# A cross-attention and GELU kernel: the exponential's table and one block pair moved ahead, one sum and one product moved back

## The chip, the cores and the metric

The kernel runs on one core of one Trainium2 chip. The metric is the device time of one execution in microseconds (us); the figure of a kernel is the median of its runs.

## What is computed

For each of 8 batches and 8 heads, a sequence x (512 rows of 64) and a state (32 rows of 64) read each other by softmax attention. The 544 rows of a batch, heads side by side, then go through two matrix products with an exact GELU between them.

```python
def _attn_ref(x, state):                  # x: (8, 8, 512, 64), state: (8, 8, 32, 64)
    scores = scale * np.matmul(x, state.transpose(0, 1, 3, 2))
    # ... softmax over the 32 states gives a
    xread = np.matmul(a, state)
    scores2 = scale * np.matmul(state, x.transpose(0, 1, 3, 2))
    # ... softmax over the 512 rows gives a2
    sread = np.matmul(a2, x)
    return np.concatenate([xread, sread], axis=2)

def _moe_ref(x, w_in, w_out):             # x: (4352, 512), w_in: (512, 2048), w_out: (2048, 512)
    h = x @ w_in
    g = 0.5 * h * (1.0 + erf(h * inv_sqrt2))
    return g @ w_out
```

## The kernel before

Batches are worked in turn. The kernel never forms xread: it multiplies each head's state by its rows of w_in first (`p_mm`, giving P), and the hidden layer of a batch is then P by the transposed attention weights AT. Block m of 16 is 128 of the 2048 hidden columns (`mm1`, called in pairs by `M(16 * b + m, ...)`), and ScalarE's GELU takes it from PSUM. So a batch needs, in order: its x in SBUF (`load_x`), rearranged by GpSimd (`rearr`) and transposed by a DMA (`xtr_dma`); the scores and their exponential (`scores`); the division by the row sums (`norm`, called "scaling" here); the weights transposed by a DMA (`atr_dma`); then its 16 blocks.

The second product of batch 0 is done in units of four matmuls (`U(12)` to `U(15)` are the last of it). That of later batches is done with seven half-size products in place of eight, after Strassen: VectorE adds quadrants of g (`g_sum`) or of w_out (`w_sums`), and `X(b, name)` is one of the seven products, 16 matmuls each.

PSUM has eight banks. Four form the pool `ps_f`, tag "f", whose tiles are given out in rotation: the fifth tile takes the buffer of the first and waits until it has been read. The other four are named o0 to o3; X's seven products use them as the table in `X` says.

ScalarE holds one function table at a time, so each change between the exponential and GELU brings a table load. Each engine works through its own instructions in the order in which they are written, and engines wait for one another only where data or a buffer is shared. `hold_for` is a tiny copy on GpSimd whose only purpose is that GpSimd, which also issues the loads of x, stands still until some block's GELU is there.

```python
    xin = ctx.enter_context(tc.tile_pool(name="xin", bufs=2))
    att = ctx.enter_context(tc.tile_pool(name="att", bufs=2))
    ps_f = ctx.enter_context(tc.tile_pool(name="ps_f", bufs=4, space=PSUM))
    ps_o = ctx.enter_context(tc.tile_pool(name="ps_o", bufs=1, space=PSUM))
# ... cut ...
    def state_prep(b0, b1, pool=ps_f, tag="f"):
        n = b1 - b0
        ps = pool.tile([128, n, HC, NS], BF16, name="st_ps", tag=tag)
        for b in range(b0, b1):
            nc.tensor.transpose(
                ps[:, b - b0, :, :].rearrange("p c n -> p (c n)"),
                st_bf[:, b, :, :].rearrange("q t d -> q (t d)"),
                ident,
            )
        for t in range(2):
            nc.vector.tensor_copy(
                out=sbd[64 * t:64 * t + 64, b0:b1, :, 32 * t:32 * t + 32].rearrange(
                    "d b c n -> d (b c) n"
                ),
                in_=ps[64 * t:64 * t + 64, :, :, :].rearrange("d b c n -> d (b c) n"),
            )
# ... cut ...
    def rearr(b, ts=(0, 1)):
        A = atts[b]
        src = xbs[b].rearrange("p (t c) (j d) -> p t c j d", t=2, d=D)
        for t in ts:
            nc.gpsimd.tensor_copy(
                out=A.x4[:, :, :, 64 * t:64 * t + 64].rearrange("p j c d -> p c j d"),
                in_=src[:, t],
            )
# ... cut ...
    def xtr_dma(b):
        A = atts[b]
        nc.sync.dma_start_transpose(
            out=A.xT.rearrange("p j c n -> p (j c) n"),
            in_=A.x4.rearrange("p j c n -> p (j c n)"),
        )
# ... cut ...
    def scores(b, half):
        A = atts[b]
        if half == 0:
            begin_e(b)
        pt = ps_f.tile([128, SJ, 2, 2, NS], FP32, name="pt", tag="f")
        for ci in range(2):
            c = 2 * half + ci
            for j in range(SJ):
                nc.tensor.matmul(
                    pt[:, j, :, ci, :],
                    lhsT=A.xT[:, j, c, :],
                    rhs=sbd[:, b, c, :],
                    start=True,
                    stop=True,
                )
        nc.scalar.activation(
            out=A.e[:, :, 64 * half:64 * half + 64],
            in_=pt.rearrange("p j t c n -> p (j t) (c n)"),
            func=AF.Exp,
            scale=scale,
        )
# ... cut ...
    def norm(b, half):
        A = atts[b]
        G = SJ * 2
        hs = slice(64 * half, 64 * half + 64)
        e4 = A.e[:, :, hs].rearrange("p g (c n) -> p g c n", n=NS)
        cs = att.tile([128, G, 2], FP32, name="cs", tag="cs")
        nc.vector.reduce_sum(out=cs, in_=e4, axis=AX.X)
        ics = att.tile([128, G, 2], FP32, name="ics", tag="ics")
        nc.vector.reciprocal(out=ics, in_=cs)
        nc.vector.tensor_tensor(
            out=A.a[:, :, hs].rearrange("p g (c n) -> p g c n", n=NS),
            in0=e4,
            in1=ics[:, :, :].to_broadcast((128, G, 2, NS)),
            op=ALU.mult,
        )
# ... cut ...
    def atr_dma(b):
        A = atts[b]
        A.AT = att.tile([128, SJ, 2, 128], BF16, name="AT", tag="AT")
        nc.sync.dma_start_transpose(
            out=A.AT.rearrange("p j t n -> p (j t) n"), in_=A.a
        )
# ... cut ...
    def p_mm(b, f, tiles):
        if b not in Ps:
            Ps[b] = att.tile([128, 2, d_ff], BF16, name="P", tag="P")
        ps = [tiles([128, 512], "p_ps") for t in range(2)]
        for c in range(HC):
            for t in range(2):
                nc.tensor.matmul(
                    ps[t][32 * c:32 * c + 32, :],
                    lhsT=sbd[64 * t:64 * t + 64, b, c, 32 * t:32 * t + 32],
                    rhs=w_in_bf[64 * t:64 * t + 64, c, f * 512:(f + 1) * 512],
                    start=True,
                    stop=True,
                )
        return ps
# ... cut ...
    def p_copy(b, f, ps):
        dst = Ps[b][:, :, f * 512:(f + 1) * 512]
        nc.scalar.copy(out=dst[:, 0, :], in_=ps[0])
        nc.vector.tensor_copy(out=dst[:, 1, :], in_=ps[1])
# ... cut ...
    def mm1(b, m):
        if m == 0:
            gs[b] = gpool.tile([128, MC, S], BF16, name="g", tag="g")
        hp = ps_f.tile([128, S], FP32, name="hp", tag="f")
        for t in range(2):
            nc.tensor.matmul(
                hp,
                lhsT=Ps[b][:, t, m * 128:(m + 1) * 128],
                rhs=atts[b].AT[:, :, t, :],
                start=(t == 0),
                stop=(t == 1),
            )
        nc.scalar.activation(out=gs[b][:, m, :], in_=hp, func=AF.Gelu)
# ... cut ...
    def g_sum(b, name):
        (h0, k0), (h1, k1), op = G_SUMS[name]
        t = apool.tile([128, MH, 256], BF16, name="gsum", tag="gsum")
        nc.vector.tensor_tensor(out=t, in0=g_q(b, h0, k0), in1=g_q(b, h1, k1), op=op)
        xs[b, "g" + name] = t
# ... cut ...
    def X(b, name):
        bank = {"3": 0, "4": 1, "5": 0, "2": 1, "1": 2, "6": 3, "7": 2}[name]
        first = name in "3416"
        if first:
            xs[b, bank] = otile([128, 2, NH], "xp", bank)
        ps = xs[b, bank]
        lhs = {"3": (0, 0), "4": (1, 1)}.get(name)
        lhs = xs[b, "g" + name] if lhs is None else g_q(b, *lhs)
        rhs = {"5": w_q[1][1], "2": w_q[0][0]}.get(name)
        rhs = w_sum[name] if rhs is None else rhs
        x_mm(ps, lhs, rhs, first)
        if name == "3":
            xs[b, "s3"] = c_tile("s3")
            if b > 1:
                nc.scalar.copy(out=xs[b, "s3"], in_=ps)
# ... cut ...
    def hold_for(b, m):
        nc.gpsimd.tensor_copy(out=hold, in_=gs[b][:, m, 0:1])
# ... cut ...
# the order in which work is written, from the end of batch 0 to the start of batch 2
    mm2_m(0, 11)
    w_sums(0)
    begin(2)
    rearr(2)
    xtr_dma(2)
    hold_for(0, 15)
    load_x(3)
    load_st(3, B)
    M(18, 19)
    U(12)
    burst([(1, 2), (1, 3)])
    U(13)
    state_prep(2, 3, ps_o, "o3")
    w_sums(1)
    begin(3)
    rearr(3, (0,))
    M(20, 21)
    U(14)
    M(22, 23)
    g_sum(1, "6")
    U(15)
    scores(2, 0)
    scores(2, 1)
    X(1, "3")
    norm(2, 0)
    norm(2, 1)
    atr_dma(2)
    nc.gpsimd.tensor_copy(out=hold, in_=atts[2].a[:, 0, 64:65])
    rearr(3, (1,))
    xtr_dma(3)
    M(24, 25)
    M(26, 27)
    X(1, "6")
    homes = iter((1, 2, None, None))

    def home(shape, name):
        at = next(homes)
        return ftile(shape, name) if at is None else otile(shape, name, at)

    p0 = p_mm(2, 0, home)
    p1 = p_mm(2, 1, home)
    for f, t, ps in ((1, 0, p1), (1, 1, p1), (0, 1, p0)):
        nc.vector.tensor_copy(out=Ps[2][:, t, f * 512:(f + 1) * 512], in_=ps[t])
    M(28, 29)
    nc.scalar.copy(out=Ps[2][:, 0, 0:512], in_=p0[0])
    hold_for(1, 12)
    rearr_ones(2)
    M(30, 31)
    state_prep(3, B)
    nc.scalar.copy(out=xs[1, "s3"], in_=xs[1, 0])
    w_sums(3)

    for b in range(2, B):
        nb = b + 1
        for p in range(8):
            k = 16 * b + 2 * p
            if p == 1 and nb < B:
                scores(nb, 0)
                scores(nb, 1)
            if p in (2, 3) and nb < B:
                norm(nb, p - 2)
            if p == 3 and nb + 1 < B:
                xtr_dma(nb + 1)
            if p == 5 and nb < B:
                atr_dma(nb)
            if p == 7 and nb < B:
                srt(b)
                if nb == B - 1:
                    srt(nb)
            if nb == B and p < 5:
                read_out_slot(p)
                if p == 4:
                    r_homes()
                    r_sum("5")
                    r_sum("2")
                continue
            M(k, k + 1)
            if b == 2 and p in (0, 3):
                pmat(2, 2 + p // 3)
            if b == 2 and p == 1:
                w_sums(4)
            if p < 5:
                if p == 0:
                    g_sum(b - 1, "5")
                    if b > 2:
                        sr_w("5216"[b - 3])
                X(b - 1, "45127"[p])
                if p < 3:
                    g_sum(b - 1, "127"[p])
            if p == 0 and b + 3 < B:
                hold_for(b, 0)
                load_x(4 if b == 2 else b + 3)
# ... cut ...
```

Of the kernel before, what the change touches and what calls it, by code (L numbers as in the profile page):

```python
# [9 lines left out]
FP32 = mybir.dt.float32  # L10
# [7 lines left out]
def kernel(  # L18
# [57 lines left out]
    xT0 = persist.tile([128, 4, SJ, 128], BF16, name="xT0", tag="mix2")  # L76
    sb0 = persist.tile([128, 2, 2, 2, NS], BF16, name="sb0")
    hold = persist.tile([128, 1], BF16, name="hold")
    warm = persist.tile([128, 512], BF16, name="warm")
    xos = [persist.tile([128, SJ, HC, 132], BF16, name=f"xo_{i}") for i in range(2)]  # L80
    x4s = [persist.tile([128, SJ, HC, 128], BF16, name=f"x4_{i}") for i in range(2)]
# [15 lines left out]
    for i in range(2):  # L97
        nc.vector.memset(xos[i][:, :, :, 1:2], 1.0)
        nc.vector.memset(xos[i][:, :, :, 130:131], 1.0)

    def load_w_in(f0, f1):
        for t in range(2):
# [98 lines left out]
    atts = {}  # L201
# [16 lines left out]
# [8 lines that stand above are left out]
# [47 lines left out]
# [6 lines that stand above are left out]
# [29 lines left out]
    def norm0(t):  # L308
        A = atts[0]
        ics = att.tile([128, SJ, HC], FP32, name="ics", tag="ics")  # L310
        nc.vector.reciprocal(out=ics, in_=A.sums)
        nc.vector.tensor_tensor(
            out=A.a.rearrange("p (j t) (c n) -> p j t c n", t=2, n=NS)[:, :, t, :, :],
            in0=A.e.rearrange("p (j t) (c n) -> p j t c n", t=2, n=NS)[:, :, t, :, :],
            in1=ics[:, :, :].to_broadcast((128, SJ, HC, NS)),
            op=ALU.mult,
        )

    def scores(b, half):
        A = atts[b]  # L320
# [232 lines left out]
    def w_sums(i):  # L553
        (b11, b12), (b21, b22) = w_q
        w_add(*(
            ("3", b12, b22, ALU.subtract),
            ("4", b21, b11, ALU.subtract),
            ("6", b11, b12, ALU.add),
            ("1", b11, b22, ALU.add),
            ("7", b21, b22, ALU.add),  # L560
        )[i])
# [14 lines left out]
# [5 lines that stand above are left out]
# [34 lines left out]
# [15 lines that stand above are left out]
            for h in range(2):  # L630
                xs[b, "o", h] = hpool.tile([128, 2, d_model], FP32, name="oh", tag=f"oh{h}")
        elif name == "4":
            xs[b, "s34"] = c_tile("s34")
            nc.vector.tensor_tensor(out=xs[b, "s34"], in0=ps, in1=xs[b, "s3"], op=ALU.add)
        elif name == "5":
            o = xs[b, "o", 0][:, :, NH:]
            nc.scalar.copy(out=o, in_=ps)  # L637
            xs[b, "u"] = c_tile("u")
            x_out(b, 0, right)
            nc.gpsimd.tensor_tensor(out=xs[b, "u"], in0=xs[b, "s34"], in1=o, op=ALU.subtract)  # L640
        elif name == "2":
            nc.scalar.copy(out=xs[b, "o", 1][:, :, :NH], in_=ps)  # L642
            c22(b)
        elif name == "1":
            xs[b, "q"] = c_tile("q")
            nc.vector.tensor_tensor(out=xs[b, "q"], in0=ps, in1=xs[b, "s34"], op=ALU.add)
        elif name == "7":
            nc.vector.tensor_tensor(
                out=xs[b, "o", 0][:, :, :NH], in0=ps, in1=xs[b, "u"], op=ALU.add
            )  # L650
            x_out(b, 0, left)
# [253 lines left out]
    def hold_for(b, m):  # L905
        nc.gpsimd.tensor_copy(out=hold, in_=gs[b][:, m, 0:1])


    def M(*ms):
        for m in ms:  # L910
            mm1(m // MC, m % MC)

    def U(*us):
        for u in us:
            mm2(u // 16, u % 16 // 4, u % 4)
# [146 lines left out]
    begin(2)  # L1062
    rearr(2)
    xtr_dma(2)
    hold_for(0, 15)
    load_x(3)
    load_st(3, B)
    M(18, 19)
# [3 lines left out]
    state_prep(2, 3, ps_o, "o3")  # L1072
    w_sums(1)
    begin(3)
    rearr(3, (0,))
    M(20, 21)
    U(14)
    M(22, 23)
    g_sum(1, "6")
    U(15)  # L1080
    scores(2, 0)
    scores(2, 1)
# [2 lines left out]
    norm(2, 1)  # L1085
    atr_dma(2)
    nc.gpsimd.tensor_copy(out=hold, in_=atts[2].a[:, 0, 64:65])
    rearr(3, (1,))
    xtr_dma(3)
    M(24, 25)  # L1090
    M(26, 27)
    X(1, "6")
    homes = iter((1, 2, None, None))

    def home(shape, name):
        at = next(homes)
# [1 line left out]

    p0 = p_mm(2, 0, home)
    p1 = p_mm(2, 1, home)  # L1100
    for f, t, ps in ((1, 0, p1), (1, 1, p1), (0, 1, p0)):
        nc.vector.tensor_copy(out=Ps[2][:, t, f * 512:(f + 1) * 512], in_=ps[t])
    M(28, 29)
    nc.scalar.copy(out=Ps[2][:, 0, 0:512], in_=p0[0])
# [2 lines left out]
    M(30, 31)  # L1107
    state_prep(3, B)
    nc.scalar.copy(out=xs[1, "s3"], in_=xs[1, 0])
    w_sums(3)  # L1110

    for b in range(2, B):
        nb = b + 1
        for p in range(8):
            k = 16 * b + 2 * p
            if p == 1 and nb < B:
                scores(nb, 0)
                scores(nb, 1)
            if p in (2, 3) and nb < B:
# [14 lines that stand above are left out]
                    r_sum("2")  # L1134
                continue
            M(k, k + 1)
            if b == 2 and p in (0, 3):
                pmat(2, 2 + p // 3)
            if b == 2 and p == 1:
# [12 lines that stand above are left out]
            if p == 6 and b == 2:  # L1152
                hold_for(b, 12)
                load_x(5)
            if p == 0 and nb + 1 < B:
                begin(nb + 1)
                rearr(nb + 1)
            if nb == B:
                if p == 5:
                    g_sum(b, "6")  # L1160
                    R("3")
                    r_sum("1")
                    R("4")
                    r_sum("6")
                    r_sum("7")
                if p == 6:
                    R("5")
                    X(b, "3")
                    R("2")
                    R("1")  # L1170
                if p == 7:
                    R("6")
                    X(b, "6")
                continue
            if p == 5:
                g_sum(b, "6")
                reads = (b, nb) if nb == B - 1 else (b,)
                for r in reads:
                    sread(r)
                p_run(nb, (0, 1), ((0, 1), (3, 2)))  # L1180
                for r in reads:
                    sread_out(r)
                if b == 2:
                    rearr_ones(3)
                elif nb + 1 < B:
                    rearr_ones(nb + 1)
            if p == 6:
                X(b, "3")
            if p == 7:
                if b == 2:  # L1190
                    rearr_ones(4)
                p_run(nb, (2, 3), ((1, 2), None))
                X(b, "6")
# [41 lines left out]
```

The softmax here doesn't subtract the row's maximum and nothing guards it: scores larger than these inputs give would overflow.

## Time and profile before

Three runs took 204.58, 205.17 and 205.64 us; the median is 205.17. The profiled execution spans 203.2 us, at a granted TensorE clock of 0.999.

| engine | busy us | share of the span | instructions |
|---|---|---|---|
| PE, TensorE's matmuls | 196.3 | 97% | 2030 |
| PEld, TensorE's weight loads | 132.4 | 65% | 2035 |
| DVE, VectorE | 157.2 | 77% | 254 |
| ACT, ScalarE | 135.6 | 67% | 239 |
| POOL, GpSimd | 68.4 | 34% | 76 |

In the profile's lines a time in us is counted from the first instruction. A line of the timeline gives start, duration, engine, line of the program, operation, "output<-input" by the program's names, the tile and shape, and how many such instructions were merged; in brackets stands the idle time just before and what ended it. L488 is the matmul of `mm1`, L495 its GELU, L585 the matmul of `X`, L579 `g_sum`, L551 `w_sums`, L327 and L334 the matmul and the exponential of `scores`, L157 the transposition in `state_prep`, L222 `rearr`, L514 the matmul of `U`, L637 the copy in `X(b, "5")`. "ACTq" and "SPq" are the instruction queues of ScalarE and SyncE. The chain of work that ended last is followed back from the last instruction, at each step to what released it.

| group | count | mean ns |
|---|---|---|
| GELU of a block, ScalarE, 128x512 | 124 | 602 |
| table load before GELU or before the exponential, ScalarE | 14 | 1283 |
| sum of quadrants of g, VectorE, 128x2048 | 35 | 1326 |
| rearranging copy of half a batch's x, GpSimd, 128x1024 | 12 | 1081 |

Six transpositions of x by DMA landed 4.2 to 8.0 us after their issue (median 4.5), six of the weights 3.3 to 5.1 (median 3.6).

### The profile page before, as it was taken

Reading aid. Unit: us, or ns where it says so; the run is one execution under the profiler, and the core shown is the slowest. Engines: PE = TensorE matmul, PEld = TensorE weight load, DVE = VectorE, ACT = ScalarE, POOL = GpSimd, SP = SyncE. Lnnn points to the kernel's source line nnn. Section 1 sums busy time; section 2 is a strip of 40 time slices with the busy share of each in tenths; the row PEclk is TensorE's granted clock in tenths of the full one; section 3 lists DMA queues with packets and bytes.
Section 4 is the critical chain, followed back from the end, with each engine's and each line's share of the span. In section 5 each row is a group of like instructions: output and inputs, shape, how many; then the busy total and the mean of one; then the engine's idle time right before and its main releaser. Section 6 shows DMA issues by size and latency. Waiting matters only on the chain.

```text
span 203.2 us, 4895 instructions
## 1 busy us (share of the span) xinstructions
PE 196.3 (97%) x2030; PEld 132.4 (65%) x2035; DVE 157.2 (77%) x254; ACT 135.6 (67%) x239; POOL 68.4 (34%) x76
## 2 busy tenths in 40 slices
PE   7899999999899999999999999999999999999993
PEld 2434544465577577766776677667775787878893
DVE  2954876788998979978897787768778988895882
ACT  3785678688985779566967696687847576864020
POOL 8973204324439546370627502430220002200000
PEclk9999999999999999999999999999999999999999
DMA  6999997994785788755783405750107001040135
GB/s 189 191 174 203 205 199 117 147 244 110 113 142 103 209 106 106 155 168 42 81 180 119 91 0 128 116 127 0 52 10 200 3 0 55 0 158 0 52 103 160
DMA packets 40566, 23.16 MB, mean 114 GB/s; under 512 B 21856, under 2 KB 39136, under 8 KB 40544
## 3 DMA queue, kind: packets, MB, share of 16 engines
q0 software_dynamic: 13984, 8.10, 29.9%
q1 hardware_dynamic: 25872, 14.36, 28.4%
q10 hardware_dynamic: 688, 0.39, 0.6%
q8 instruction: 16, 0.26, 0.5%
q14 instruction: 6, 0.05, 0.1%
HBM read 17.30 MB, written 8.91 MB: 129 GB/s over the span
## 4 chain that ended last, share of the span: by engine, by line
PE 73%; DMA 16%; POOL 5%; ACT 3%; issue 1%; DVE 0%; POOLq 0%
PE xp L585 39%; PE hp L488 21%; DMA xb<-in_x_dram 11%; DMA xT<-x 4%; PE p_ps L423 3%; PE sp L792 3%; PE rp L858 3%; POOL w_in_bf L103 2%; PE xp L697 2%; DMA AT<-a 2%; PE pt L327 1%; PE sr L386 1%; POOL x L222 1%; ACT g L495 1%; POOL sbd L94 1%
## 5 line engine op out<-in xcount | busy, mean ns | idle before, releaser
L495 ACT ACTIVATE g<-hp 128x512 bf16<-128x512 f32 x124 | 67.2, 602 | 27.4 <-PE hp L488 20.8
L488 PE MATMUL hp<-AT,P 128*128 128x512 bf16 x248 | 63.0, 379 | 0.8 <-DMA AT<-a 0.8
L585 PEld LDWEIGHTS <-gsum 128*128 128x128 bf16 x528 | 51.1, 98 | 12.4 <-issue 1.9
L579 DVE TENSOR_TENSOR gsum<-g 128x2048 bf16<-128x2048 bf16 x35 | 45.9, 1326 | 0.1
L488 PEld LDWEIGHTS <-P 128*128 128x128 bf16 x248 | 22.8, 98 | 21.4 <-issue 3.2
L585 PE MATMUL xp<-ws,gsum 128*128 128x256 bf16 x304 | 36.3, 273 | 0.0
L585 PE MATMUL xp<-ws,g 128*128 128x256 bf16 x224 | 26.8, 273 | 0.0
L585 PE MATMUL xp<-w_out_bf,gsum 128*128 128x256 bf16 x224 | 26.6, 273 | 0.0
L585 PEld LDWEIGHTS <-g 128*128 128x128 bf16 x224 | 21.7, 98 | 4.6 <-issue 0.2
L640 POOL TENSOR_TENSOR u<-s,oh 128x512 f32<-128x512 f32 x6 | 8.9, 1491 | 40.7 <-ACT oh L637 40.7
L435 DVE CAST P<-p_ps 128x512 bf16<-128x512 f32 x29 | 18.8, 684 | 3.0 <-PE p_ps L423 2.9
L222 POOL COPY x<-xb 128x1024 bf16<-128x1024 bf16 x12 | 12.7, 1081 | 21.9 <-DMA xb<-in_x_dram 21.9
L434 ACT CAST P<-p_ps 128x512 bf16<-128x512 f32 x29 | 15.8, 598 | 5.4 <-PE p_ps L423 5.1
L232 POOL COPY xo<-xb 128x1024 bf16<-128x1024 bf16 x12 | 14.6, 1245 | 4.5 <-PE sr L386 4.5
L604 POOL TENSOR_TENSOR v<-q,oh 128x512 f32<-128x512 f32 x6 | 8.7, 1456 | 20.5 <-ACT oh L642 20.3
L530 PE MATMUL op<-w_out_bf,g 128*128 128x512 bf16 x44 | 11.1, 380 | 0.5 <-issue 0.3
L350 DVE TENSOR_TENSOR a<-e,ics 128x512 bf16<-128x512 bf16 x14 | 10.4, 745 | 0.5
L347 DVE TENSOR_REDUCE cs<-e 128x16 f32<-128x512 bf16 x14 | 9.5, 677 | 1.4 <-ACT e L334 1.4
L423 PE MATMUL p_ps<-w_in_bf,sbd 64*32 64x512 bf16 x248 | 10.3, 382 | 0.0
L413 DVE COPY XSR<-srT 128x128 bf16<-128x128 bf16 x8 | 5.7, 758 | 5.3 <-PE srT L410 5.3
L334 ACT ACT_TABLE_LOAD x7 | 9.0, 1283 | 0.9 <-issue 0.8
L495 ACT ACT_TABLE_LOAD x7 | 9.0, 1283 | 0.1
(129 smaller groups left out, 224.8 us busy)
## 6 DMA issues: line engine op xcount, KB each, us to landing
out_dram<-oh SPq DMA_DIRECT2D x15, 256.0 KB, 2.5
xb<-in_x_dram POOLq DMA_DIRECT2D x7, 512.0 KB, 5.9
out_dram<-oh SPq DMA_DIRECT2D x6, 512.0 KB, 3.0
w_in_bf<-in_moe_w_in_dram POOLq DMA_DIRECT2D x6, 256.0 KB, 11.0
out_dram<-osb SPq DMA_DIRECT2D x5, 256.0 KB, 5.4
w_out_bf<-in_moe_w_out_dram POOLq DMA_DIRECT2D x4, 256.0 KB, 8.1
w_out_bf<-in_moe_w_out_dram POOLq DMA_DIRECT2D x2, 512.0 KB, 12.8
x0f<-in_x_dram SPq DMA_DIRECT2D x3, 256.0 KB, 3.9
```

Of the source, the lines that this page charges most:

```text
L222: nc.gpsimd.tensor_copy(out=A.x4[:, :, :, 64 * t:64 * t + 64].rearrange("p j c d -> p c j d"), in_=src[:, t],)
L232: eng.tensor_copy(out=A.xo[:, :, :, 2 + 64 * t:66 + 64 * t].rearrange("p j c d -> p c j d"), in_=src[:, t],)
L347: nc.vector.reduce_sum(out=cs, in_=e4, axis=AX.X)
L350: nc.vector.tensor_tensor(out=A.a[:, :, hs].rearrange("p g (c n) -> p g c n", n=NS), in0=e4, in1=ics[:, :, :].to_broadcast((128, G, 2, NS) ...
L423: nc.tensor.matmul(ps[t][32 * c:32 * c + 32, :], lhsT=sbd[64 * t:64 * t + 64, b, c, 32 * t:32 * t + 32], rhs=w_in_bf[64 * t:64 * t + 64, c ...
L434: nc.scalar.copy(out=dst[:, 0, :], in_=ps[0])
L435: nc.vector.tensor_copy(out=dst[:, 1, :], in_=ps[1])
L488: nc.tensor.matmul(hp, lhsT=Ps[b][:, t, m * 128:(m + 1) * 128], rhs=atts[b].AT[:, :, t, :], start=(t == 0), stop=(t == 1),)
L495: nc.scalar.activation(out=gs[b][:, m, :], in_=hp, func=AF.Gelu)
L530: nc.tensor.matmul(ops[b, j], lhsT=gs[b][:, m, j * 128:(j + 1) * 128], rhs=w_out_bf[:, m, :], start=(m == 0), stop=(m == MC - 1),)
L579: nc.vector.tensor_tensor(out=t, in0=g_q(b, h0, k0), in1=g_q(b, h1, k1), op=op)
L585: nc.tensor.matmul(ps[:, j - js[0], :], lhsT=lhs[:, m, 128 * j:128 * j + 128], rhs=rhs[:, m, :], start=(first and j == js[0] and m == 0), ...
```

## The change

All of it lies between the end of batch 0 and the start of batch 3. It concerns what batch 2's attention waits for, and what stands on each engine ahead of it.

- The load of batch 3's x is released when batch 2's transposed x has landed, and no longer by the last GELU of batch 0; it then doesn't share the DMA engines with that transposition.
- An exponential of a spare 128x1 tile stands ahead of unit 14, so that the exponential's table is loaded before batch 2's scores are ready. For that, the pair of blocks 22 and 23 moves ahead of unit 14, so that no GELU lies between.
- The quadrant sum 6 of batch 1 moves from before batch 2's scores to behind its scaling, and batch 3's x is rearranged in one go behind the scaling.
- Product 6 of batch 1 (`X(1, "6")`) moves behind batch 1's last blocks. Its bank o3 is thereby free for a P tile: three of the four P tiles of batch 2 now lie in o1, o3 and o2, one in the rotating pool, and their casts come in another order.
- In batch 2's second slot, blocks 34 and 35 come ahead of batch 3's scores.

```diff
--- before.py
+++ after.py
@@ -76,6 +76,7 @@
     xT0 = persist.tile([128, 4, SJ, 128], BF16, name="xT0", tag="mix2")
     sb0 = persist.tile([128, 2, 2, 2, NS], BF16, name="sb0")
     hold = persist.tile([128, 1], BF16, name="hold")
+    spare = persist.tile([128, 1], FP32, name="spare")
     warm = persist.tile([128, 512], BF16, name="warm")
     xos = [persist.tile([128, SJ, HC, 132], BF16, name=f"xo_{i}") for i in range(2)]
     x4s = [persist.tile([128, SJ, HC, 128], BF16, name=f"x4_{i}") for i in range(2)]
@@ -97,6 +98,7 @@
     for i in range(2):
         nc.vector.memset(xos[i][:, :, :, 1:2], 1.0)
         nc.vector.memset(xos[i][:, :, :, 130:131], 1.0)
+    nc.vector.memset(spare, 0.0)
 
     def load_w_in(f0, f1):
         for t in range(2):
@@ -315,6 +317,9 @@
             in1=ics[:, :, :].to_broadcast((128, SJ, HC, NS)),
             op=ALU.mult,
         )
+
+    def exp_table():
+        nc.scalar.activation(out=spare, in_=spare, func=AF.Exp)
 
     def scores(b, half):
         A = atts[b]
@@ -1062,7 +1067,7 @@
     begin(2)
     rearr(2)
     xtr_dma(2)
-    hold_for(0, 15)
+    nc.gpsimd.tensor_copy(out=hold, in_=atts[2].xT[:, 0, 0, 0:1])
     load_x(3)
     load_st(3, B)
     M(18, 19)
@@ -1072,11 +1077,10 @@
     state_prep(2, 3, ps_o, "o3")
     w_sums(1)
     begin(3)
-    rearr(3, (0,))
     M(20, 21)
+    M(22, 23)
+    exp_table()
     U(14)
-    M(22, 23)
-    g_sum(1, "6")
     U(15)
     scores(2, 0)
     scores(2, 1)
@@ -1085,12 +1089,12 @@
     norm(2, 1)
     atr_dma(2)
     nc.gpsimd.tensor_copy(out=hold, in_=atts[2].a[:, 0, 64:65])
-    rearr(3, (1,))
+    rearr(3)
     xtr_dma(3)
+    g_sum(1, "6")
     M(24, 25)
     M(26, 27)
-    X(1, "6")
-    homes = iter((1, 2, None, None))
+    homes = iter((1, 3, 2, None))
 
     def home(shape, name):
         at = next(homes)
@@ -1098,7 +1102,7 @@
 
     p0 = p_mm(2, 0, home)
     p1 = p_mm(2, 1, home)
-    for f, t, ps in ((1, 0, p1), (1, 1, p1), (0, 1, p0)):
+    for f, t, ps in ((1, 1, p1), (0, 1, p0), (1, 0, p1)):
         nc.vector.tensor_copy(out=Ps[2][:, t, f * 512:(f + 1) * 512], in_=ps[t])
     M(28, 29)
     nc.scalar.copy(out=Ps[2][:, 0, 0:512], in_=p0[0])
@@ -1107,13 +1111,14 @@
     M(30, 31)
     state_prep(3, B)
     nc.scalar.copy(out=xs[1, "s3"], in_=xs[1, 0])
+    X(1, "6")
     w_sums(3)
 
     for b in range(2, B):
         nb = b + 1
         for p in range(8):
             k = 16 * b + 2 * p
-            if p == 1 and nb < B:
+            if p == 1 and 3 < nb < B:
                 scores(nb, 0)
                 scores(nb, 1)
             if p in (2, 3) and nb < B:
@@ -1134,6 +1139,9 @@
                     r_sum("2")
                 continue
             M(k, k + 1)
+            if b == 2 and p == 1:
+                scores(nb, 0)
+                scores(nb, 1)
             if b == 2 and p in (0, 3):
                 pmat(2, 2 + p // 3)
             if b == 2 and p == 1:
```

## The prediction

> **What bounds the kernel now.** I read the chain of work that ended last first. From 51.41 us to its last piece it is TensorE work end to end: whatever reaches that point earlier ends earlier, unless a new gap opens. Ahead of it, three waits (columns: start us, length us, what):
>
> ```profile
> 34.08 7.71 DMA xT<-x
> 41.78 0.81 issue
> 42.60 1.28 ACT L334
> 43.88 0.01 issue
> 43.89 1.08 ACT e L334 x2
> ...
> 48.04 3.33 DMA AT<-a
> 51.37 0.04 issue
> 51.41 1.02 PE hp L488 x4
> ```
>
> The reader sees the transposed x of batch 2 take 7.71 us to land, the exponential's table load stand behind the scores, and TensorE wait at 51.41 for the transposed weights AT. The TensorE timeline tells what these cost it:
>
> ```profile
> 40.93 1.03 PE L514 MATMUL op<-w_out_bf,g 128*128 128x512 bf16 x4
> 42.12 0.64 PE L327 MATMUL pt<-sbd,xT 128*128 128x64 bf16 x16 [0.17 <-DMA xT<-x]
> ...
> 50.21 0.44 PE L157 MATMUL st_ps<-ident,st_bf 128*128 128x128 bf16 x5
> 51.41 1.02 PE L488 MATMUL hp<-AT,P 128*128 128x512 bf16 x4 [0.76 <-DMA AT<-a]
> ```
>
> Ends are modelled, so I count from starts. Groups of this form start 0.87 apart, so the scores could have started at 40.93 + 0.87 = 41.80: 0.32 lost. The five transposes take about 0.3 by start spacing, so block 32 could start at 50.5: 0.9 lost. Together 1.2 us, all that this stretch has to give.
>
> **The table load.** The instructions of the scores' line around it (durations min/median/max, then first and last start):
>
> ```profile
> L334 ACTq EVENT_SEMAPHORE  x1: 1434/1434/1434, 41.1 to 41.1; - x1
> L334 ACT ACT_TABLE_LOAD  x1: 1283/1283/1283, 42.6 to 42.6; - x1
> ```
>
> ScalarE's queue waits from 41.1 in an instruction of its own, and the load stands behind it. For batch 3 there is none and the load starts at 53.68, ahead of its scores at 54.47.
>
> **What the Trainium skill says.** "ScalarE: Activation LUTs", section What ACT_TABLE_LOAD costs, gives about 1283 ns a load, which the trace repeats, and 186 ns plus 0.833 ns an element for a plain activation, hence an estimate of 0.19 us for the spare one. The 1380 ns of drain it adds do not show: the load at 45.00 starts 0.02 after the exponentials. "SBUF — State Buffer", section Who interferes with whom: a VectorE operation with two SBUF inputs and a GpSimd operation reading SBUF exclude each other for a whole instruction, the first to start winning. The trace agrees where the VectorE and GpSimd timelines meet:
>
> ```profile
> 76.81 2.02 POOL L222 COPY x<-xb 128x1024 bf16<-128x1024 bf16 x2
> ```
> ```profile
> 77.08 2.84 DVE L579 TENSOR_TENSOR gsum<-g 128x2048 bf16<-128x2048 bf16 x1
> ```
>
> The sum, 1.22 us elsewhere, ends 1.1 after both copies. "Trainium Kernel Development and Optimization", Key Constraints: transfers of all queues share 16 DMA engines and interleave. That fits 7.71 us for the transposition beside load_x(3), against the 4.4 us landing of batch 3's.
>
> **The change, part by part.**
>
> *Release by xT.* load_x(3) waits for batch 2's transposition instead of gelu 15. The transposition should land near 34.08 + 4.4 = 38.5, well before 41.80: the 0.32 goes. load_x(3) moves from 35.75 to about 38.8; with the 5.9 us median landing, slowed by output transfers, it is in at 45 to 46.5. That is early enough, since rearr(3) now waits for batch 2's scaling anyway.
>
> *Pair 22, 23 ahead of unit 14, and the spare exponential.* TensorE reaches gelu blocks 20 to 23 at 38.34 without a break. A gelu starts 0.63 after its pair (38.34 to 38.97), four take 2.06 (row at 46.29), so ScalarE is done at 41.03; load to 42.33; spare to about 42.55. The scores start at 41.80 and are ready 0.43 later, so the real exponential starts at 42.55 instead of 43.89: 1.34 earlier.
>
> *g_sum 6 behind the scaling.* The scaling ends 4.0 after the exponential's start (43.89 to 47.89), so at 46.55, and AT is issued at 46.70 and lands at 50.0 (3.33 as before). The quadrant sum follows at once at 46.5, about 0.2 ahead of GpSimd's next read, so it should take the shared port and run its 1.22; GpSimd waits. The casts of P stand behind it: sum to cast spacing 1.14, cast 0.68, so the first ends at 48.33.
>
> *Homes and unit of seven.* Only one P tile is in the four-buffer pool now. Following the rotation by hand, block 31 takes that buffer. TensorE: scores 41.80, X3 42.26, blocks 24 to 27 at 44.01, P products at 45.84, blocks 28, 29, 30 at 46.40, 46.83, 47.26, block 31 ready at 47.70. It must wait for the cast until 48.38: 0.68 of a new gap. Then 0.43 (block 31), 0.29 (transposes) and 1.75 (X6) give block 32 at 50.85. AT has been there since 50.0. Against 51.41: 0.56 gained.
>
> *Pair 34, 35 ahead of batch 3's scores.* Before, the table loads stood ahead of those gelus; now they fall between 35 and 36. The rows before:
>
> ```profile
> 57.38 1.09 ACT L495 ACTIVATE g<-hp 128x512 bf16<-128x512 f32 x2
> 58.35 0.60 ACT L637 COPY oh<-xp 128x512 f32<-128x512 f32 x1
> 58.81 1.12 ACT L495 ACTIVATE g<-hp 128x512 bf16<-128x512 f32 x2
> ```
>
> Let T be the start of pair 34. ScalarE: 0.63 to the first gelu, pair 1.09, load 1.30, exponentials to the start of the copy 0.97, copy 0.59, load back 1.32 with its gaps, gelu pair 1.11: gelu 37 ends at T + 7.01. By the rotation the second tile of pmat(2,3) takes gelu 37's buffer. TensorE gets there after pair, scores, X5, pair, X1, pair: 0.87 + 0.46 + 1.74 + 0.87 + 1.74 + 0.96 = T + 6.64. The new gap is about 0.39 with the release. Before, gelu 37 ended at 59.93 and TensorE came at 61.11.
>
> The sum: -0.32 - 0.9 + 0.68 + 0.39, rounded terms included, is -0.56 + 0.39 = -0.17. From 205.17 this is 205.0.
>
> **Rivals.** *All the waits go and none comes*: 205.17 - 1.2 = 204.0. For it speaks that AT is in time; against it the order of VectorE's queue, sum before cast, and the buffer count. *The port goes the other way*: if GpSimd's copies start first, the sum ends near 46.75 + 2.02 + 1.14 = 49.9, the cast at 50.6, block 32 at 53.1: +1.7, and 207.2 with the later gap. The sum has only about 0.2 of a lead; I give this one in ten. *The late load becomes the wait*: the states of batches 3 to 7 were issued at 36.62 and took 9.9; issued near 39.7 and as slow they land at 49.6, against the transposes at 48.8: +0.8, or 205.8. With the transposition out of the way they should be faster. *Batch 3's xT*: GpSimd copies start at about 47.8 instead of 48.14 and 44.70, so xT(3) is issued near 49.9 instead of 49.38 and lands at 54.3; its scores are at 54.8, half a microsecond of slack. *Port again*: w_sums(3) now meets rearr_ones(2) and may end near 53.3, which brings g_sum 5 to 55.0, against X5 at 55.2.
>
> **Range and chances.** Two gains that I trust (1.2) stand against two gaps that I had to count by hand, each good to perhaps 0.3; the three repeats of before spread by 1.06. I say 205.0, 204.2 to 206.0. Two per cent is 4.1 us, more than any of these paths holds: 0.97 for within, 0.01 faster, 0.02 slower.
>
> **What would show it.** xT landing before 40 and no wait at the scores; a table load on L334 near 41.0; exponential at 42.5; AT issued near 46.7; a wait of 0.7 at block 31 on the cast of P; block 32 near 50.9 without a wait for AT; a wait of 0.4 at pmat(2,3) on a gelu; TensorE closed after that. Wrong if the sum of quadrants takes over 2 us, if the state transposes wait for a transfer, or if batch 3's scores wait for xT.

## The result, and the profile after

The changed kernel takes 207.96 us (median of six executions, 207.06 to 209.92) against 205.04: a ratio of 1.0149, 95% interval 1.0101 to 1.0197. Measured a second time it came to 207.3, ratio 1.0108 (1.0050 to 1.0166). It is slower by 1 to 1.5 per cent. I had said 205.0, and 206.0 at the most.

The chain of work that ended last (start, length, what) has lost all three waits of before and has one new link:

```profile
40.69 10.49 DMA st_bf<-in_state_dram
```

It is the load of the states of batches 3 to 7, issued at 40.69 and landed at 51.2. Lines of the program stand two to five further down than before: L493 is the block's matmul and L500 its GELU, L590 the matmul of `X`, L159 the state transposition, L332 and L339 the scores and their exponential, L322 the spare one, L355 the scaling, L428 the P product and L1106 its casts, L584 `g_sum`, L224 `rearr`, L117 and L121 the loads of x and of the states. TensorE's timeline:

```profile
41.69 0.63 PE L332 MATMUL pt<-sbd,xT 128*128 128x64 bf16 x16
...
46.28 1.04 PE L493 MATMUL hp<-AT,P 128*128 128x512 bf16 x4
48.06 1.02 PE L493 MATMUL hp<-AT,P 128*128 128x512 bf16 x4 [0.75 <-DVE P L1106]
51.22 0.45 PE L159 MATMUL st_ps<-ident,st_bf 128*128 128x128 bf16 x5 [2.14 <-DMA st_bf<-in_state_dram]
...
53.26 1.03 PE L493 MATMUL hp<-AT,P 128*128 128x512 bf16 x4
...
62.96 0.81 PE L428 MATMUL p_ps<-w_in_bf,sbd 64*32 64x512 bf16 x8
63.70 1.92 PE L590 MATMUL xp<-w_out_bf,gsum 128*128 128x256 bf16 x16
```

The wait for xT is gone. A wait on a cast of P is there, as predicted; then 2.14 for the states, which the prediction had as a rival of 0.8 and as a sign of being wrong, but not in its sum. Block 32 starts at 53.26 instead of 51.41. At pmat(2,3), the last quarter of batch 2's P, TensorE's timeline before was:

```profile
61.11 0.41 PE L423 MATMUL p_ps<-w_in_bf,sbd 64*32 64x512 bf16 x8
61.45 1.92 PE L585 MATMUL xp<-w_out_bf,gsum 128*128 128x256 bf16 x16
```

There it was 0.34 to the next start, and it is 0.74 now: a gap of 0.40, where 0.39 was predicted. The product behind it runs 2.25 late (63.70 against 61.45); the whole span is 2.1 longer. ScalarE's timeline, where the gain was meant to come from:

```profile
40.95 1.28 ACT L322 ACT_TABLE_LOAD   x1
42.24 0.20 ACT L322 ACTIVATE spare<-spare 128x1 f32<-128x1 f32 x1
42.35 1.06 ACT L339 ACTIVATE e<-pt 128x512 bf16<-128x512 f32 x2
```

The table load moved as meant, the spare exponential costs 0.20 and the real one starts at 42.35 instead of 43.89. The gain was made, and then spent. GpSimd's timeline shows how late its loads have become:

```profile
39.29 0.19 POOL L1070 COPY hold<-xT 128x1 bf16<-128x1 bf16 x1 [4.77 <-DMA xT<-x]
39.81 0.88 POOL L117 DMA_DIRECT2D xb<-in_x_dram  x1 [0.34 <-PE hp L493]
40.69 0.95 POOL L121 DMA_DIRECT2D st_bf<-in_state_dram  x1
46.41 1.05 POOL L1091 COPY hold<-a 128x1 bf16<-128x1 bf16 x1 [4.77 <-DVE a L355]
48.35 2.02 POOL L224 COPY x<-xb 128x1024 bf16<-128x1024 bf16 x2 [0.89 <-DMA xb<-in_x_dram]
```

The states are issued at 40.69, 4.07 later than before:

```profile
36.62 0.95 POOL L119 DMA_DIRECT2D st_bf<-in_state_dram  x1
```

The one-element copy at 46.41 takes 1.05: it started 0.22 after the quadrant sum and ended with it, the way round that the prediction chose. VectorE, in the same stretch, loses nothing to it:

```profile
46.19 1.22 DVE L584 TENSOR_TENSOR gsum<-g 128x2048 bf16<-128x2048 bf16 x1
47.33 1.88 DVE L1106 CAST P<-p_ps 128x512 bf16<-128x512 f32 x3
```

### The profile page after: what moved, and what is told of

Its sections match the earlier page's. It is cut to its first block, busy times and chain, and to the rows that moved or that the text cites. A ratio compares the mean times of both kernels' runs of the same rounds, so it can differ in the third digit from the quotient of the medians.

```text
span 205.3 us, 4901 instructions
## 1 busy us (share of the span) xinstructions
PE 197.2 (96%) x2035; PEld 132.6 (65%) x2035; DVE 157.1 (77%) x255; ACT 135.7 (66%) x240; POOL 68.7 (33%) x76
## 4 chain that ended last, share of the span: by engine, by line
PE 89%; DMA 7%; DVE 1%; ACT 1%; POOL 0%; issue 0%
PE xp L590 40%; PE hp L493 25%; PE op L535 5%; DMA st_bf<-in_state_dram 5%; PE p_ps L428 4%; PE sp L797 3%; PE rp L863 3%; PE xp L702 2%; DMA st_f<-in_state_dram 2%; PE pt L332 1%; PE sr L391 1%; PE op L519 1%; PE hp L1008 1%; PE aT_ps L373 1%; PE xT_ps L270 0%; DVE x0b L242 0%
## 5 line engine op out<-in xcount | busy, mean ns | idle before, releaser
L500 ACT ACTIVATE g<-hp 128x512 bf16<-128x512 f32 x124 | 67.0, 603 | 30.5 <-PE hp L493 23.8
L493 PE MATMUL hp<-AT,P 128*128 128x512 bf16 x248 | 63.0, 379 | 0.8 <-DVE P L1106 0.7
L590 PEld LDWEIGHTS <-gsum 128*128 128x128 bf16 x528 | 50.9, 98 | 11.9 <-issue 2.1
L584 DVE TENSOR_TENSOR gsum<-g 128x2048 bf16<-128x2048 bf16 x35 | 45.9, 1324 | 0.1
L493 PEld LDWEIGHTS <-P 128*128 128x128 bf16 x248 | 22.8, 98 | 21.6 <-issue 3.6
L590 PE MATMUL xp<-ws,gsum 128*128 128x256 bf16 x304 | 36.3, 273 | 0.0
L590 PE MATMUL xp<-ws,g 128*128 128x256 bf16 x224 | 26.7, 273 | 0.0
L590 PE MATMUL xp<-w_out_bf,gsum 128*128 128x256 bf16 x224 | 26.6, 273 | 0.0
L590 PEld LDWEIGHTS <-g 128*128 128x128 bf16 x224 | 21.7, 98 | 4.6 <-issue 0.2
L224 POOL COPY x<-xb 128x1024 bf16<-128x1024 bf16 x12 | 12.6, 1078 | 15.8 <-DMA xb<-in_x_dram 15.8
L535 PE MATMUL op<-w_out_bf,g 128*128 128x512 bf16 x48 | 11.8, 380 | 0.0
L428 PE MATMUL p_ps<-w_in_bf,sbd 64*32 64x512 bf16 x248 | 10.7, 382 | 0.0
L355 DVE TENSOR_TENSOR a<-e,ics 128x512 bf16<-128x512 bf16 x14 | 10.3, 734 | 0.5
L617 DVE TENSOR_TENSOR oh<-xp,v 128x512 f32<-128x512 f32 x6 | 4.1, 690 | 5.5 <-POOL v L609 5.5
```

The lines of the kernel that those rows point to most:

```text
L224: nc.gpsimd.tensor_copy(out=A.x4[:, :, :, 64 * t:64 * t + 64].rearrange("p j c d -> p c j d"), in_=src[:, t],)
L355: nc.vector.tensor_tensor(out=A.a[:, :, hs].rearrange("p g (c n) -> p g c n", n=NS), in0=e4, in1=ics[:, :, :].to_broadcast((128, G, 2, NS) ...
L428: nc.tensor.matmul(ps[t][32 * c:32 * c + 32, :], lhsT=sbd[64 * t:64 * t + 64, b, c, 32 * t:32 * t + 32], rhs=w_in_bf[64 * t:64 * t + 64, c ...
L493: nc.tensor.matmul(hp, lhsT=Ps[b][:, t, m * 128:(m + 1) * 128], rhs=atts[b].AT[:, :, t, :], start=(t == 0), stop=(t == 1),)
L535: nc.tensor.matmul(ops[b, j], lhsT=gs[b][:, m, j * 128:(j + 1) * 128], rhs=w_out_bf[:, m, :], start=(m == 0), stop=(m == MC - 1),)
L590: nc.tensor.matmul(ps[:, j - js[0], :], lhsT=lhs[:, m, 128 * j:128 * j + 128], rhs=rhs[:, m, :], start=(first and j == js[0] and m == 0), ...
```

## The experiments

Two questions: is it the states' load that costs, and if so, why does it hurt here? Theories 1 to 3 of the first four runs: only the late states; the late release as a whole, with AT delayed too; the reordering. All times are medians, with the ratio to the kernel before on the same chip.

**The states ahead of the release.**

```diff
     xtr_dma(2)
+    load_st(3, B)
     nc.gpsimd.tensor_copy(out=hold, in_=atts[2].xT[:, 0, 0, 0:1])
     load_x(3)
-    load_st(3, B)
```

> The changed kernel with one move: the load of the states of batches 3 to 7 is issued ahead of the wait for batch 2's transposed x; the load of x of batch 3 still waits. Theory 1 (the late state load alone is what the prediction missed): the 2.14 us wait at the state transposes goes, block 32 starts near 50.9 and the time is 205.0 to 205.6. Theory 2 (the whole late release collides with what follows, and AT is late too, hidden behind the state wait): AT still lands near 52, block 32 waits for it by about 1.2, and the time is 206.0 to 206.8. Theory 3 (the reordering on TensorE and VectorE costs the time): no wait worth naming moves, 207 to 208.

Measured 209.28, ratio 1.0173 (1.0139 to 1.0207). TensorE's timeline:

```profile
52.02 1.02 PE L493 MATMUL hp<-AT,P 128*128 128x512 bf16 x4 [0.65 <-DMA AT<-a]
...
58.12 0.64 PE L332 MATMUL pt<-sbd,xT 128*128 128x64 bf16 x16 [2.02 <-DMA xT<-x]
```

The wait for the states is gone, but the states now share the DMA engines with batch 2's transposition, which takes 8.0 instead of 4.7. So the release comes at 42.10, batch 3's x lands at 51.0, AT is awaited for 0.65 and batch 3's xT for 2.02. AT lands at 52.0, which is theory 2's point, but no theory had the rest: the move only passed the lateness on to x, and so tells little of what the late states alone cost.

**The old release in the changed kernel.**

```diff
-    nc.gpsimd.tensor_copy(out=hold, in_=atts[2].xT[:, 0, 0, 0:1])
+    hold_for(0, 15)
```

> The changed kernel with the release of before: the load of batch 3's x and of the states waits for gelu 15 again. Theories 1 and 2: no state wait, AT lands near 50.1, batch 2's xT near 41.8, block 32 at about 51, a gap of 0.4 at pmat(2,3): 204.8 to 205.4. Theory 3: the release is innocent and the time stays above 206.5.

Measured 206.1, ratio 1.0029 (1.0011 to 1.0048). The states' wait is gone and most of the loss with it, so theory 3 falls. What is left, a little more than expected, are recorded waits of 0.52 for batch 2's xT, 0.58 for the cast and 0.43 for batch 3's xT.

**The new release in the kernel before.**

```diff
-    hold_for(0, 15)
+    nc.gpsimd.tensor_copy(out=hold, in_=atts[2].xT[:, 0, 0, 0:1])
```

> The kernel before with the new release alone. Theory 1: the states land near 51.2 against transposes due at 49.9, which the wait for AT mostly hid before: 205.1 to 205.8. Theory 2: AT, issued near 47.7, takes 5 to 6 us behind the late loads and lands near 53.3, block 32 is 1.9 later than before: 206.5 to 207.5. Theory 3: the release is innocent, 204.7 to 205.2.

Measured 205.57, ratio 0.9999 (0.9971 to 1.0027). On its own the release is harmless: the states, issued at 40.44, took 9.0 and landed at 49.4, and their transposes, which stand behind product 6 there, come only at 49.92, without a wait:

```profile
49.92 0.44 PE L157 MATMUL st_ps<-ident,st_bf 128*128 128x128 bf16 x5
```

The loss needs the release and the rest of the change together.

**The spare exponential and the pair 22, 23 in the kernel before.**

```diff
     M(20, 21)
-    U(14)
     M(22, 23)
+    exp_table()
+    U(14)
```

> The kernel before with the spare exponential and blocks 22 and 23 ahead of unit 14, nothing else. Theories 1 and 2: the exponential starts about 1.2 earlier, AT is issued near 47.1 and lands near 50.4, block 32 starts about 0.9 earlier and no new gap comes: 204.0 to 204.4. Theory 3: the order of blocks and units itself costs, 205.0 or more.

Measured 205.08, ratio 0.9990 (0.9969 to 1.0012): no difference that can be told, where I expected 0.9 us. In the profiled execution batch 2's xT takes 7.1, the scores start only at 42.52, and GpSimd's copy of batch 3's x stretches the last scaling step from 0.69 to 1.09.

**Release, exponential and pair together, nothing else.** Theory A: AT's transposition, issued earlier, and the late loads get in each other's way. Theory B: it is only that product 6 no longer stands ahead.

```diff
-    hold_for(0, 15)
+    nc.gpsimd.tensor_copy(out=hold, in_=atts[2].xT[:, 0, 0, 0:1])
...
-    U(14)
     M(22, 23)
+    exp_table()
+    U(14)
```

> The kernel before with the new release, the spare exponential and blocks 22, 23 ahead of unit 14; product 6, the sum and the casts stay where they were. Theory A (the earlier transposition of AT, 46.4 instead of 47.7, runs into the late loads, slows them and is slowed): the states land at 50.5 to 51.2 against transposes due at 49.8, AT takes over 4.5, block 32 waits 0.5 to 1.2: 204.9 to 206. Theory B (the late state load hurts only because product 6 no longer stands ahead of the state transposes): both land in time, all of the 1.2 that I counted is gained: 203.9 to 204.4.

Measured 205.66, ratio 1.0014 (0.9991 to 1.0037). TensorE's timeline:

```profile
50.63 0.45 PE L159 MATMUL st_ps<-ident,st_bf 128*128 128x128 bf16 x5 [0.40 <-DMA st_bf<-in_state_dram]
51.66 1.02 PE L493 MATMUL hp<-AT,P 128*128 128x512 bf16 x4 [0.57 <-DMA AT<-a]
```

Both waits are there with product 6 in its old place, as theory A has it. The states took 10.3 and AT 4.5. But the states cost 0.57 by starts here (50.63 against 50.06) and 2.29 in the changed kernel. Of the 1.72 between, 1.13 is that the transposes are due earlier there (48.93), since product 6 no longer stands ahead, and 0.59 that the states come later. So the larger part of it comes of moving product 6, which is theory B's point; no run undid that move alone in the changed kernel.

**The changed kernel without the spare exponential.**

```diff
     M(22, 23)
-    exp_table()
     U(14)
```

> The changed kernel without the spare exponential, so that the real one starts near 43.5 and AT is issued about 1.1 later. Theory A: the states land near 49.5 instead of 51.2, AT takes about 3.5, and taking away this gain makes the kernel faster: 206.3 to 207.3 against 208.0. Theory B: the states land where they did, and the casts come later on top: 208 to 209.

Measured 206.87, ratio 1.0099 (1.0074 to 1.0125), where theory A put it. But the times do not decide for theory A: the executions of the changed kernel at a full clock have a median of 206.84, the same as here, and none of the five here was at 0.992, as half of the changed kernel's were. What they show is that the spare exponential gains nothing in this place. The wait for the states was 0.84 and AT took 3.3. Part of that is the moment of issue, 39.97 there. The states issued at nearly that moment in the second profile of the changed kernel (39.94) took 10.2 against 9.8, and AT, issued 1.06 earlier, took 4.8. That is 0.4 and 1.5 in one pair of executions; the 0.4 is less than the states differ by between other executions.

**Batch 3's state early, the others later.** Only 32 KB, loaded with batch 2's; the transposes of 4 to 7 move into batch 2.

```diff
-        load_st(2, 3)
+        load_st(2, 4)
...
-    load_st(3, B)
...
-    state_prep(3, B)
+    state_prep(3, 4)
...
                 load_x(4 if b == 2 else b + 3)
+                if b == 2:
+                    load_st(4, B)
...
+            if p == 4 and b == 2:
+                state_prep(4, B)
```

> The changed kernel with batch 3's state (32 KB) loaded early, together with batch 2's, and the states of batches 4 to 7 loaded and transposed in batch 2. If the state load alone is what the prediction missed: no wait at the state transposes, block 32 at 50.3 to 50.9, the gap of 0.4 at pmat(2,3) stays: 204.6 to 205.4. If the late load of x is a second cause: AT lands after 51, or batch 3's xT after its scores, and 0.5 to 1.5 more: 205.5 to 206.8.

Measured 205.42, ratio 1.0006 (0.9984 to 1.0028). TensorE's timeline:

```profile
42.27 0.63 PE L332 MATMUL pt<-sbd,xT 128*128 128x64 bf16 x16
...
51.31 1.03 PE L493 MATMUL hp<-AT,P 128*128 128x512 bf16 x4
...
61.01 0.80 PE L428 MATMUL p_ps<-w_in_bf,sbd 64*32 64x512 bf16 x8
```

With the states out of the way the whole loss is gone, and the rest of my working nearly holds: L428 keeps its gap, and from the scores to block 32 it is 9.04, predicted 50.85 - 41.80 = 9.05. That they agree so closely is luck: the wait on the cast was 0.92 by starts instead of 0.68, and one state transposition took 0.05 where I had five in 0.29. AT took 3.9 and was in time. Theory 1, then, is enough for the loss; AT's delay stayed hidden behind the wait for the states.

**The same with batch 3's scores ahead of blocks 34 and 35.**

```diff
-            if p == 1 and 3 < nb < B:
+            if p == 1 and nb < B:
...
-            if b == 2 and p == 1:
-                scores(nb, 0)
-                scores(nb, 1)
```

> The run state_split with batch 3's scores ahead of blocks 34 and 35 again, as in the kernel before. If the gap of 0.4 at pmat(2,3) comes from ScalarE's order (two table loads between gelus 35 and 36): it is gone, but batch 3's xT, which landed at 54.9 there, is awaited at the scores for about 0.5: 205.2 to 205.8. If the gap has another cause it stays and adds to that wait: 205.8 to 206.4.

Measured 205.66, ratio 1.0010 (0.9988 to 1.0032). L428 is back at its old length, 0.41 against 0.80. So that gap does come from the order of tables and gelus. The scores hardly wait for xT in this execution (they start at 54.78, about 0.15 after they could), so the order of the change bought little for its 0.4; the medians do not tell the two apart.

**Four attempts at a better kernel.** "best" is the kernel before with the edits of release_exp and those of state_split:

> The kernel before with new release, spare exponential, blocks 22, 23 ahead of unit 14, and the state load split as in the run state_split; no other part of the change. If the split takes away the collision: AT lands near 50.4, block 32 starts near 50.3 to 50.5, batch 3's xT in time: 203.9 to 204.5. If x of batch 3 alone is late enough to hold AT or the scores of batch 3: 204.8 to 206.

It took 205.9, ratio 1.0037 (1.0008 to 1.0067), single executions reaching 209.7. Its profiled execution was 0.73 ahead at batch 3's scores (53.74 against 54.47) and lost part again: the moved transposes, hidden in the wait for AT before, now stand in the open at 65.10. In the end its span is 203.3, as before (203.2), at a mean clock of 0.996. The spread I cannot explain.

The next runs place the release between the two, at gelu 19, first in the changed kernel:

```diff
-    nc.gpsimd.tensor_copy(out=hold, in_=atts[2].xT[:, 0, 0, 0:1])
+    M(18, 19)
+    hold_for(1, 3)
     load_x(3)
     load_st(3, B)
-    M(18, 19)
```

> The changed kernel with a release between the old and the new one: the loads of batch 3's x and of the states wait for gelu 19, which ends near 36.7, so that they are issued about 2.3 earlier than in the changed kernel and 1.2 later than in the kernel before. If the moment of the release alone makes the 2.1 wait: states land before 48.9, AT takes under 4, block 32 near 51, gap at pmat(2,3) 0 to 0.4: 204.8 to 205.6. If the loads run into batch 2's transposition as with the old release, xT lands after 42 and it is 205.8 to 206.3, as that run was.

It took 205.97, ratio 1.0025 (1.0008 to 1.0043). x of batch 2 landed late in that execution and the states, issued at 39.23, took 11.5; they were awaited for 0.57. The earlier release helps by about one per cent, and not all the way. Then in "best", with ScalarE's cast of P ahead of blocks 28 and 29 as well:

```diff
+    nc.scalar.copy(out=Ps[2][:, 0, 0:512], in_=p0[0])
     M(28, 29)
-    nc.scalar.copy(out=Ps[2][:, 0, 0:512], in_=p0[0])
```

> The run best with the release by gelu 19 and ScalarE's cast of P ahead of gelus 28 and 29. If what was left there were the 0.3 wait on that cast and the 0.4 wait for batch 3's xT: block 32 starts near 50.0, no wait at the scores of batch 3, 203.9 to 204.6. If the x load slows batch 2's transposition again: 204.8 to 205.6.

It took 205.56, ratio 1.0003 (0.9984 to 1.0022): batch 3's x took 11.5 to land in the profiled execution, and the scores waited 3.09 for xT. And with the split of the states undone (`load_st(2, 3)`, `load_st(3, B)` and `state_prep(3, B)` as before):

> The same without the split of the state load: the kernel before with spare exponential, blocks 22 and 23 ahead of unit 14, release by gelu 19 and the early cast. The states, issued near 38, land near 47.5 to 48.5, ahead of their transposes at 49.3, and AT behind them near 50 to 50.5: 203.9 to 204.7. If states and AT collide again: a wait for AT of 0.5, 204.8 to 205.4.

It took 204.86, ratio 0.9981 (0.9966 to 0.9996), with a wait of 0.84 for AT although AT took only 3.3. GpSimd's copy and VectorE's scaling meet again:

```profile
46.46 1.04 POOL L224 COPY x<-xb 128x1024 bf16<-128x1024 bf16 x1 [6.88 <-DMA xb<-in_x_dram]
```
```profile
46.50 1.54 DVE L355 TENSOR_TENSOR a<-e,ics 128x512 bf16<-128x512 bf16 x1
```

**The copy out of the scaling's way.**

```diff
-    rearr(3, (0,))
...
-    rearr(3, (1,))
+    rearr(3)
```

> The kernel gelu19_cast with batch 3's x rearranged in one go behind batch 2's scaling, as in the changed kernel. If the shared port made AT late there: the last scaling step takes 0.7 again, AT is issued about 0.85 earlier, the wait for AT shrinks from 0.84 to under 0.3: 203.9 to 204.5, provided that batch 3's xT, issued near 49.5, lands before its scores. If the transfers made it late: AT takes over 4 or is no earlier, 204.7 to 205.3.

Measured 204.72, ratio 0.9967 (0.9948 to 0.9985): the fastest kernel here, and with gelu19_cast one of the two that come out ahead of the kernel before, by 0.3 and 0.2 per cent. TensorE's timeline:

```profile
51.27 1.04 PE L493 MATMUL hp<-AT,P 128*128 128x512 bf16 x4 [0.46 <-DMA AT<-a]
```

The last scaling step takes 0.69 again, AT is issued 0.77 earlier (47.43 against 48.20), and half of the wait goes. AT takes 3.8 now, so the transfers have a part in what is left, and the time came out 0.2 above what I expected.

**The changed kernel a second time.**

> The changed kernel unaltered, measured a second time. If the long wait for the states brings TensorE's clock down in some executions: median 207.3 to 208.5, a third or more of the executions at a mean clock of 0.992, these about 1 us longer than those at 1.0. If the first six were chance: under a tenth at 0.992, median 206.8 to 207.3.

Measured 207.3. The profiled execution waits 1.08 for the states, half of what the first profile showed. Two of six executions had a mean TensorE clock of 0.992, against four of six in the first measurement: median and share lie just at the edge of the first expectation, and the two were some 2 us longer than the others, not 1.

## Why the prediction was wrong

*Release by xT.* The step that failed: that the late loads come in time and cost nothing. The transposition landed as said (4.7 after its issue). But load_x(3) went out at 39.81, not 38.8, because batch 2's x was half a microsecond later in this execution and GpSimd needed about another half for the hold and the issue; and x landed after 8.5, at 48.3, not at 45 to 46.5. I had taken the median landing of 5.9, which belongs to loads with less beside them: while the load of 53.34 was under way in the kernel before, 90 GB/s were moved in all, against 153 from 39.8 to 48.3 here. And that x was early enough for rearr(3) said nothing of the states, which are issued behind it and which TensorE needs sooner.

*The rival "the late load becomes the wait".* Right in kind, wrong in size. I had 39.7 + 9.9 = 49.6 against transposes due at 48.8, called that 0.8, and then set it aside with the words that the loads "should be faster" without the transposition beside them. They were issued at 40.69 and took 10.5, and the transposes were due at 48.06 + 0.87 = 48.93. So TensorE lost 51.22 - 48.93 = 2.29 by starts: about 1.0 more than the 0.8 from the later issue and 0.6 from the longer flight, less 0.1. That term stood with 0 in my sum and is nearly all of the error in the profiled span.

*Why they were no faster.* In five executions with the new release and the old order of loads (release_only, release_exp, after_no_exp, the changed kernel twice) x took 7.9 to 8.5, against 8.9 to 9.8 with the old release (before, exp_only, old_release): a little faster, as I had said. The states took 9.0 to 10.5 against 9.5 to 10.9, hardly so. They stand behind x in GpSimd's queue, and landed 2.9 after it in the changed kernel; ahead of x, in st_first, they took 6.9. The output transfers were beside them as before. The Trainium skill, "DMA: Bandwidth & Descriptors", section Queues, rings and completion order, says that each DMA engine takes turns between its queues packet by packet; that a queue which joins slows the others is my inference, and no run here takes the output transfers away.

*The states and AT.* That the states' load delays AT is shown, by single executions: with it AT took 5.8 and 4.8 in the changed kernel and 4.5 in release_exp, without it 3.9 (state_split) and 3.1 (best). In the four profiles in which AT took over 4 beside the states it landed 1.0 to 1.1 after them. That AT delays the states, the other half of theory A, is not shown: they took 9.9 and 9.5 in before and old_release, where they had landed when AT was issued, 10.9 in exp_only, where the two overlapped by 0.2, and 10.6 in gelu19_cast, where they overlapped by 1.0; with an overlap of 3.5 to 4.8, in release_exp and the changed kernel, it was 10.2 to 10.5.

*Table load and exponential.* Right: 42.35 against 42.55.

*g_sum 6 behind the scaling.* Right: the sum had the port first and took 1.22. AT was issued at 46.43 (46.70 predicted). Its landing, 52.2 instead of 50.0, is wrong, and hidden.

*Homes and unit of seven.* Right in kind: 0.91 lost by starts (48.06 against 46.28 + 0.87 = 47.15), 0.68 predicted. But it was block 30 that waited, not 31. Why is open: in after_no_exp, one line apart, block 31 started at 48.39 although the first cast ran from 48.38 to 49.06, so the rotation as it was counted, with the fifth tile taking the buffer of the first, does not fit what either kernel did.

*Pair 34, 35.* Right: 0.40, predicted 0.39.

The sum with what was measured: -0.56 for block 32 as predicted, 2.29 for the states, 0.23 more for the cast and 0.40 at pmat(2,3), less 0.11 by which this execution was ahead at the scores (41.69 against 41.80), give 2.25. That is what the two traces show at the product behind pmat(2,3).

## What to carry to other kernels

When a load is moved behind an event, follow everything issued after it on the same queue, the small load too, to its first reader, and ask whether that reader moves earlier in the same change: here the load went 4 us later and its reader 1.3 us earlier. Take a landing time from loads in the same company, not the median of the kernel. And a gain on one engine is worth only what the next wait leaves of it.

## What the runs showed of the hardware

Of the twelve executions of the changed kernel six had a mean granted clock of 0.992, median 208.56, the others about 1.0, median 206.84. Of the kernel before, 7 of 192 measured beside the experiments were at 0.992 or lower. 0.008 of 206 us is 1.65 us, which is near the difference of 1.72. The Trainium skill, "TensorE: Matmul & The Clock Gate", section Part 1: The HAM clock gate, has the clock halve after an idle window of about 3.4 us; one window of that length at half speed loses half of it, an estimate of 1.7. But no profiled execution caught the drop, and the waits recorded are shorter than such a window. Nor did a wait bring it about where one was profiled: executions that waited 2.14 (the changed kernel), 2.02 (st_first) and 3.09 (gelu19_split) had mean clocks of 1.000, 0.998 and 0.998. So the cause stays open. The slower executions do account for the median lying further from the kernel before (2.9) than the profiled span (2.1), which is that of an execution at full clock.

Which of GpSimd's copy and VectorE's scaling step goes first can hang on 0.04 us: in gelu19_cast the copy started at 46.46, the step at 46.50, and the step took 1.54 instead of the 0.69 of gelu19_rearr, where the copy came behind it.
